# Linformer attention and a maxout feed-forward on one core: row maxima subtracted inside PSUM, and later keys transposed by TensorE

## The chip, the core and the metric

The kernel runs on one core of a Trainium2 chip. Times are microseconds (us) of device time for one execution. The kernel before takes 319.98 us (median of three runs, 319.91 to 320.13). TensorE appears in the profile as PE (matmuls) and PEld (weight loads), VectorE as DVE, ScalarE as ACT, GpSimd as POOL and SyncE as SP.

## The reference

```python
batch, n_heads, seq, head_dim = (8, 8, 1024, 64)      # k_proj = 64
def _attn_ref(q, k, v, E, F):
    k_proj = np.einsum('ks,bhsd->bhkd', E, k)
    v_proj = np.einsum('ks,bhsd->bhkd', F, v)
    scores = q @ k_proj.transpose(0, 1, 3, 2) / np.sqrt(q.shape[-1])
    scores = scores - np.max(scores, axis=-1, keepdims=True)
    attn = np.exp(scores)
    attn = attn / (np.sum(attn, axis=-1, keepdims=True) + 1e-09)
    return np.matmul(attn, v_proj)

# x: attention's output as 8192 tokens by 512
def _moe_ref(x, w1, w2, w_out):                       # 512x1024, 512x1024, 1024x512
    return np.maximum(x @ w1, x @ w2) @ w_out
```

The query of a token is compared with 64 projected keys, so a row of scores has 64 entries. The row's maximum cancels in the quotient; it only bounds the argument of the exponential.

## The kernel before

The kernel goes through the 8 batches. A batch's attention is cut into four *groups* `(g, j)`: four heads (`g`) by half the tokens (`j`), `W` = 256 columns each for even and odd tokens (`o`). The feed-forward works on *units* `(b, o)`, two per batch. Both matrix products of a unit use seven block products instead of eight (`p1` to `p7`, in `up_steps` for the first product and `down_steps` for the second). Most `up` products are copied to SBUF by ACT (`keep`, L676) or combined by DVE (`add`, L717), and the block sums that the next products need are formed by DVE (L662). `max(x@w1, x@w2) @ w_out` is computed with the difference of the two weights (`wd_sb`) and a relu, plus `x` times a product of weights (`m_sb`).

One group of attention is:

- `score` (L327): 16 small matmuls of 64 rows by 32 columns, `kpt` (keys, transposed) against `qt` (queries, transposed), 256 columns moving. The result has keys over partitions and tokens along the row, in two PSUM banks.
- an exponential on ACT out of PSUM (`scores`, L427; `step_sc`, L374 for the first groups). No maximum is subtracted.
- `sums_into` and `values_into` (both through `tiles_into`, L346): denominators (8 small matmuls with ones) and weighted values (16).
- logarithm and exponential of the negative on ACT (L448, L452), which gives the reciprocal of the denominators, and one multiply on DVE (L456) that writes the group's part of `xt`.

In the steady part `step_group` (L409) issues the scores of one group right beside denominators and values of the group before. `step_later` hands out the rest: logarithm, reciprocal, multiply.

Keys and values are projected in `step_kv` (batch 0, and batches 3 to 7 with `dma=True`) or `step_kv_sets` (batches 1 and 2). For batches 3 to 7 the projected keys are copied twice side by side and transposed by a DMA on SP's queue (`step_kpt_dma`, L291); batches 1 and 2 transpose on TensorE (`step_kpt_sets`, L254) and copy with one DVE instruction (L258). Queries are transposed by TensorE for batches 0 and 1 (`step_qt`, L305, copied by DVE at L310) and by DMA on SP's queue after that (`step_qt_dma`, L317). On POOL's queue a one-element copy from a transposed tile (`step_gate`, L297) holds back the loads of the next batch until the transposes by DMA are done.

PSUM has eight banks: four single ones named `mm0` to `mm3` (`mm_bank`) and two pairs with the tag `att` (`att_banks`).

The order of all work is written out by hand. The list `slots` holds the feed-forward's pieces in the order in which they are issued, each with a key: `("U", n, h, i)` is the `i`-th up product of half `h` (a half holds seven of them) while unit `n` does its down products, `("P", n, p, i)` a piece of down product `p`, `("G", n, h)` the start of a half, where `step_group` sits. `at_slot` hangs a step of attention behind such a key. A step that returns a function has it called after the next slot: that is how a copy out of PSUM is issued one slot behind its matmuls. Each engine takes its instructions in this order.

A batch covers two units, hence four halves, hence four groups. Units 3, 5, 7, 9 and 11 (`kv_units`) begin with the projection of keys and values of batches 3 to 7.

Of the kernel before, what the change touches and what calls it, by code (L numbers as in the profile page):

```python
# [16 lines left out]
def kernel(  # L17
# [33 lines left out]
    soft = ctx.enter_context(tc.tile_pool(name="soft", bufs=5))  # L51
    opool = ctx.enter_context(tc.tile_pool(name="opool", bufs=14))
    ppool = ctx.enter_context(tc.tile_pool(name="ppool", bufs=4))
# [52 lines left out]

    tiles = {b: {} for b in range(B)}
    for n in ("k", "q", "v"):
# [45 lines left out]


    eft = [const.tile([128, NC, KP], FP16, tag=f"eft{i}", name=f"eft{i}") for i in range(2)]

# [12 lines left out]
    def new_attn(t):  # L170
        t["kp"] = proj.tile([KP, H, 2, D], FP16, tag="kp", name="kp_sb")
        t["vp"] = proj.tile([128, H, 2, D // 2], FP16, tag="vp", name="vp_sb")
        t["kpt"] = proj.tile([128, H, KP], FP16, tag="kpt", name="kpt_sb")
        t["qt"] = qtp.tile([128, H, HALF], FP16, tag="qt", name="qt_sb")


    def step_kv(t, h0=0, h1=H, which="kv", att=False, dma=False, copy=nc.vector.tensor_copy, between=None):
        kv_ps = att_banks()[:, 0, :] if att else mm_bank(n=0 if dma else None)
        n = (h1 - h0) * D
        both = which == "v"  # L180
        nh = 2 if both else h1 - h0
        for h in range(0, h1 - h0, nh):
            if h and between is not None:
                between()
            for c in range(NC):
                for w in which:
                    i = "kv".index(w)
                    for r in range(2) if both else (i,):
                        nc.tensor.matmul(  # L189
                            out=kv_ps[r * KP : (r + 1) * KP, h * D : (h + nh) * D],  # L190
                            lhsT=eft[i][:, c, :],
                            rhs=t[w][:, h0 + h : h0 + h + nh, c, :],
                            start=(c == 0), stop=(c == NC - 1),
                        )
        zd = lambda ap: ap.rearrange("p (h d z) -> p h z d", d=D // 2, z=2)
        if "k" in which:
            eng = nc.vector.tensor_copy if which == "k" or dma else nc.scalar.copy
            kp = t["kp"][:, h0:h1]
            eng(out=kp[:, :, 0, :], in_=kv_ps[0:KP, 0:n].rearrange("p (h d) -> p h d", d=D))
        if both:  # L200
            copy(out=t["vp"][:, h0:h1], in_=zd(kv_ps[:, 0:n]))
        elif "v" in which:
            def finish_v():
                nc.vector.tensor_copy(out=t["vp"][KP:128, h0:h1], in_=zd(kv_ps[KP:128, 0:n]))
                if dma:
                    nc.vector.tensor_copy(out=kp[:, :, 1, :], in_=kp[:, :, 0, :])
                    step_kpt_dma(t)
                else:
                    step_vp(t, h0, h1)

            if att:
                return finish_v
            finish_v()


    def step_vp(t, h0=0, h1=H):
        fl = lambda ap: ap[:, h0:h1].rearrange("p h z d -> p (h z d)")
        nc.vector.tensor_copy(out=fl(t["vp"][0:KP]), in_=fl(t["vp"][KP:128]))


    ORDER = (0, 2, 1, 3)

    def step_kv_sets(t):
        bank = att_banks()[:, 0, :]
# [12 lines left out]
        k_ps = bank[:, 0:n].rearrange("p (h d) -> p h d", d=D)  # L237
        nc.scalar.copy(out=kp[:, 0 : H // 2, :], in_=k_ps)
        nc.scalar.copy(out=kp[:, H // 2, :], in_=k_ps[:, 0, :])
# [9 lines left out]
        return finish_v  # L249

    def step_kpt_sets(t):
        kpt_ps = att_banks(FP16)[:, 0, :]
        for i, a in enumerate(ORDER):
# [3 lines left out]
            )  # L257
        nc.vector.tensor_copy(  # L258
            out=t["kpt"].rearrange("q h k -> q (h k)"), in_=kpt_ps[:, 0 : H * KP]
        )  # L260

    def kpt_of(t, head, o):
        rows = t["kpt"][o * D : (o + 1) * D]
        if "sets" not in t:
            return rows[:, head]
        s, m = divmod(head, H // 2)
        return rows[:, 2 * ORDER.index((m - o) % (H // 2)) + s]

# [6 lines left out]
    def step_kpt(t, h0=0, h1=H, att=False):  # L275
        kpt_ps = att_banks(FP16)[:, 0, :] if att else mm_bank(FP16)
        for h in range(h0, h1):
            for r in range(2):
                nc.tensor.transpose(
                    out=kpt_ps[r * D : (r + 1) * D, (h - h0) * KP : (h - h0 + 1) * KP],  # L280
                    in_=t["kp"][:, h, 0, :],
                    identity=ident16[:KP, :KP],
                )
        nc.vector.tensor_copy(
            out=t["kpt"][:, h0:h1, :].rearrange("q h k -> q (h k)"),
            in_=kpt_ps[:, 0 : (h1 - h0) * KP],
        )


    def step_kpt_dma(t):  # L290
        nc.sync.dma_start_transpose(  # L291
            out=t["kpt"], in_=t["kp"].rearrange("p h r d -> p (h r d)")
        )

# [30 lines left out]
    Z = D // 2  # L325

    def score(t, g, j, banks):  # L327
        for h in range(2):
            for o in range(2):
                for e in range(2):  # L330
                    head = 4 * g + 2 * h + e
                    for s in range(2):
                        pos = D * (o ^ e) + s * Z
                        nc.tensor.matmul(  # L334
                            out=banks[e][pos : pos + Z, h * W : (h + 1) * W],
                            lhsT=kpt_of(t, head, o)[:, s * Z : (s + 1) * Z],
                            rhs=t["qt"][o * D : (o + 1) * D, head, j * W : (j + 1) * W],
                            start=True, stop=True,
                        )
        t["ex", g, j] = soft.tile([128, 2, HALF], FP16, tag="soft", name="ex_sb")  # L340
# [582 lines left out]
    step_qt(t, 0, 4, NI // 2, NI)  # L923
    warm(2)
    step_sc(t, 0, 0)
    step_sc(t, 0, 1)
    warm(2)
    step_kv(t, 4, 8, "k")
    step_dn(t, 0, 0)
    warm(2)  # L930
    step_kpt(t, 4, 8)
    step_dn(t, 0, 1)
    step_inv(t, 0, 0)
    step_inv(t, 0, 1)
    warm(2)
    step_qt(t, 4, 4, 0, NI // 2)
    step_qt(t, 4, 4, NI // 2, NI)
    warm(2)
    step_sc(t, 1, 0)
    step_kv(t, 0, 2, "v")  # L940
    step_kv(t, 2, 4, "v")
    step_dn(t, 1, 0)
    step_sc(t, 1, 1)
# [96 lines left out]
    for n, x in enumerate((  # L1040
        "", "", "", "", "", "kv", "", "kpt", "qt00 qt10", "", "sc00 sc10", "qt01",
        "qt11 dn00 in00 dn10 in10", "", "", "at00 AT10 sc01",
    )):
        key = ("P", n // 15, (n - 1) // 2 % 7, (n - 1) % 2) if n else (0, 22)
        for name in x.split():
# [6 lines left out]
            else:  # L1052
                g, j = int(name[2]), int(name[3])
                s_ = {"qt": step_qt, "sc": step_sc,
                      "dn": step_dn, "in": step_inv, "at": step_at, "AT": step_at}[name[:2]]
                args = (4 * g, 4, 2 * j, 2 * j + 2) if name[:2] == "qt" else (g, j)
# [13 lines left out]
    at_slot(("U", 1, 0, 1), step_kv_sets, t)  # L1070
    at_slot(("U", 1, 0, 4), step_kpt_sets, t)
    at_slot(("P", 0, 6, 0), step_qt_dma, t, H // 2, H)
# [3 lines left out]
    for b in range(3, B):  # L1076
# [5 lines left out]
        at_slot(key, step_qt_dma, t, H // 2, H)  # L1082
        at_slot(("G", n, 0), step_kv, t, 0, H, "kv", False, True)
        at_slot(("U", n, 0, 2), step_vp, t)
        at_slot(("U", n, 0, 6), step_gate, t, "qt", H - 1)
        at_slot(("U", n, 0, 6), step_gate, t, "kp", H - 1, 1)
        at_slot(("U", n, 0, 6), loads, b + 1, "k", "v", "q")
    for n, h in (3, 1), (4, 0), (4, 1), (5, 1), (6, 0), (6, 1), (7, 1), (8, 0):
        at_slot(("U", n, h, 3), lambda: held.pop(0)())
    groups = [(tiles[b], g, j) for b in range(1, B) for j in range(2) for g in range(2)][2:]  # L1090
    none = (None, None, None)
    for i, (new, old) in enumerate(zip([*groups[1:], none], groups)):
        n, h = divmod(i + 2, 2)
# [72 lines left out]
```

## Time and profile before

| | |
|---|---|
| median of three runs | 319.98 us (319.91 to 320.13) |
| the profiled execution | 319.73 us, its span 318.0 us |
| ACT COPY L676, 128x512 f32 out of PSUM | 592 ns, 179 times |
| DVE TENSOR_TENSOR L717, 128x512, one operand in PSUM | 688 ns, 56 times |
| DVE TENSOR_TENSOR L456, 128x1024, one operand in PSUM | 1219 ns, 26 times |
| DVE TENSOR_TENSOR L662, 128x1024 f16 / 128x512 f16 | 683 / 419 ns |
| key transposes by DMA (`kpt_sb<-kp_sb`) | 5, 2.9 us each to landing |
| query transposes by DMA (`qt_sb<-q_sb`) | 12, 5.1 us each to landing |
| stores of the output | 256 KB each, 2.7 us to landing |

The busy time of a matmul in the profile overlaps with that of its neighbours, because matmuls are pipelined: a 256-column matmul is listed with 273 ns, but in a row of them one starts every 0.109 us. Paces are therefore read from the start times. A few per cent of matmul records can be missing. On DVE, too, a queued instruction starts a little before the listed end of the one before it. In the timeline a line shows its start, its length, the engine, the line of the kernel, the operation and the tiles, and in brackets how long the engine was idle before and for whom.

### The profile page before, as it was taken

Reading aid. Unit: us, or ns where it says so; the run is one execution under the profiler, and the core shown is the slowest. Engines: PE = TensorE matmul, PEld = TensorE weight load, DVE = VectorE, ACT = ScalarE, POOL = GpSimd, SP = SyncE. Lnnn points to the kernel's source line nnn. Section 1 sums busy time; section 2 is a strip of 40 time slices with the busy share of each in tenths; the row PEclk is TensorE's granted clock in tenths of the full one; section 3 lists DMA queues with packets and bytes.
Section 4 is the critical chain, followed back from the end, with each engine's and each line's share of the span. In section 5 each row is a group of like instructions: output and inputs, shape, how many; then the busy total and the mean of one; then the engine's idle time right before and its main releaser. Section 6 shows DMA issues by size and latency. Waiting matters only on the chain.

```text
span 318.0 us, 9177 instructions
## 1 busy us (share of the span) xinstructions
PE 312.1 (98%) x3920; PEld 253.5 (80%) x3920; DVE 240.4 (76%) x437; ACT 206.1 (65%) x372; POOL 40.0 (13%) x63
## 2 busy tenths in 40 slices
PE   8989999999999999999999999999999999999996
PEld 3555588788887888788887888788887888888885
DVE  2366888877969696996969696996969696969683
ACT  2476843777776777477776778477776777765541
POOL 8269002003000300030000400040000000000000
DMA  7999999999969899899989999989969131303124
GB/s 184 203 200 197 204 206 203 207 180 157 205 119 197 152 217 245 212 182 172 237 196 213 165 200 244 221 154 179 235 142 207 45 102 35 101 33 102 35 99 132
DMA packets 76424, 53.41 MB, mean 168 GB/s; under 512 B 29536, under 2 KB 76000, under 8 KB 76384
## 3 DMA queue, kind: packets, MB, share of 16 engines
q0 software_dynamic: 30688, 28.05, 56.4%
q1 hardware_dynamic: 45408, 24.58, 32.2%
q8 instruction: 30, 0.49, 0.6%
q10 hardware_dynamic: 288, 0.20, 0.2%
q14 instruction: 10, 0.08, 0.1%
HBM read 57.15 MB, written 16.78 MB: 233 GB/s over the span
## 4 chain that ended last, share of the span: by engine, by line
PE 92%; DMA 4%; POOL 1%; ACT 1%; DVE 0%; issue 0%; POOLq 0%; DVEq 0%
PE mm_ps L794 47%; PE mm_ps L702 27%; PE mm_ps L481 4%; DMA v_sb<-in_v_dram 4%; PE att_ps L346 3%; PE mm_ps L189 3%; PE mm_ps L334 2%; PE mm_ps L590 2%; PE att_ps L231 1%; PE mm_ps L305 1%; POOL k_sb L102 0%; POOL q_sb L102 0%; ACT ld_sb L382 0%; ACT ex_sb L374 0%; DVE o_sb L892 0%; PE att_ps L513 0%
## 5 line engine op out<-in xcount | busy, mean ns | idle before, releaser
L676 ACT COPY p_sb<-mm_ps 128x512 f32<-128x512 f32 x179 | 101.8, 592 | 49.4 <-PE mm_ps L702 27.6
L794 PEld LDWEIGHTS <-big 128*128 128x128 f16 x768 | 73.6, 98 | 11.8 <-issue 3.6
L794 PE MATMUL mm_ps<-T_sb,big 128*128 128x256 f16 x576 | 76.9, 273 | 0.0
L717 DVE TENSOR_TENSOR gt_sb<-mm_ps,p_sb 128x512 f16<-128x512 f32 x56 | 38.5, 688 | 43.9 <-PE mm_ps L702 43.6
L702 PE MATMUL mm_ps<-big,big 128*128 128x256 f16 x336 | 50.4, 273 | 0.0
L702 PEld LDWEIGHTS <-big 128*128 128x128 f16 x448 | 43.8, 98 | 5.1
L794 PE MATMUL mm_ps<-wo_sb,gt_sb 128*128 128x256 f16 x256 | 42.6, 273 | 0.0
L794 PEld LDWEIGHTS <-gt_sb 128*128 128x128 f16 x376 | 35.7, 98 | 6.7 <-issue 2.7
L427 ACT ACTIVATE ex_sb<-mm_ps 128x512 f16<-128x512 f32 x50 | 27.2, 596 | 18.0 <-PE mm_ps L334 12.3
L702 PEld LDWEIGHTS <-wd_sb 128*128 128x128 f16 x336 | 32.9, 98 | 3.8
L702 PE MATMUL mm_ps<-xt_sb,wd_sb 128*128 128x256 f16 x224 | 32.8, 273 | 0.0
L456 DVE TENSOR_TENSOR xt_sb<-att_ps,ld_sb 128x1024 f16<-128x1024 f32 x26 | 31.7, 1219 | 0.2
L794 PE MATMUL mm_ps<-m_sb,xt_sb 128*128 128x256 f16 x128 | 24.4, 273 | 0.0
L824 DVE TENSOR_TENSOR o_sb<-mm_ps,p_sb 128x512 f32<-128x512 f32 x32 | 21.9, 683 | 2.8 <-ACT p_sb L853 2.0
L297 POOL COPY junk<-qt_sb 1x1 f16<-1x1 f16 x6 | 1.5, 246 | 175.1 <-DMA qt_sb<-q_sb 175.1
L720 DVE TENSOR_SCALAR gt_sb<-gt_sb 128x512 f16<-128x512 f16 (+1 forms) x60 | 21.5, 359 | 2.1
L662 DVE TENSOR_TENSOR big<-gt_sb 128x1024 f16<-128x1024 f16 x32 | 21.9, 683 | 0.0
L794 PE MATMUL mm_ps<-wo_sb,big 128*128 128x256 f16 x128 | 21.5, 273 | 0.0
L763 ACT ACTIVATE gt_sb<-mm_ps 128x512 f16<-128x512 f32 x28 | 16.8, 601 | 5.7 <-PE mm_ps L702 5.7
L794 PE MATMUL mm_ps<-T_sb,gt_sb 128*128 128x256 f16 x120 | 20.3, 273 | 0.0
L794 PEld LDWEIGHTS <-xt_sb 128*128 128x128 f16 x188 | 18.3, 98 | 2.3 <-issue 0.2
L717 DVE TENSOR_TENSOR gt_sb<-p_sb 128x512 f16<-128x512 f32 x28 | 19.1, 682 | 0.6 <-ACT p_sb L676 0.6
(113 smaller groups left out, 432.3 us busy)
## 6 DMA issues: line engine op xcount, KB each, us to landing
out_dram<-o_sb SPq DMA_DIRECT2D x62, 256.0 KB, 2.7
k_sb<-in_k_dram POOLq DMA_DIRECT2D x7, 1024.0 KB, 10.6
v_sb<-in_v_dram POOLq DMA_DIRECT2D x7, 1024.0 KB, 16.6
q_sb<-in_q_dram POOLq DMA_DIRECT2D x5, 1024.0 KB, 23.5
q_sb<-in_q_dram POOLq DMA_DIRECT2D x6, 512.0 KB, 16.2
big<-in_moe_w_dram POOLq DMA_DIRECT2D x12, 128.0 KB, 6.6
v_sb<-in_v_dram POOLq DMA_DIRECT2D x4, 256.0 KB, 13.5
wo_sb<-in_moe_w_out_dram POOLq DMA_DIRECT2D x1, 1024.0 KB, 10.8
```

What stands on the lines that cost most here:

```text
L189: nc.tensor.matmul(out=kv_ps[r * KP : (r + 1) * KP, h * D : (h + nh) * D], lhsT=eft[i][:, c, :], rhs=t[w][:, h0 + h : h0 + h + nh, c, :], ...
L427: nc.scalar.activation(out=t["ex", g, j][:, e, :], in_=banks[e], func=ACTF.Exp, scale=scale)
L456: nc.vector.tensor_tensor(out=x_out(t, g, j).rearrange("q z o n -> q o z n"), in0=at_ps.rearrange("q o (z n) -> q o z n", z=2), in1=ld[:, ...
L481: nc.tensor.matmul(out=h_ps, lhsT=wd_sb[:, r, fb * 128 : (fb + 1) * 128], rhs=t["xt"][:, r, :, j * W : (j + 1) * W], start=(r == 0), stop= ...
L662: nc.vector.tensor_tensor(out=S(i), in0=S(0) if x is None else x, in1=y(), op=op)
L676: copy(out=x, in_=bank)
L702: nc.tensor.matmul(out=bank[:, m * W : (m + 1) * W], lhsT=w_[:, n_, (2 * d + m) * 128 : (2 * d + m + 1) * 128], rhs=a[:, n_, :], start=(n ...
L717: nc.vector.tensor_tensor(out=c_blk(j, c), in0=two(x), in1=two(y), op=ALU.add)
L720: nc.vector.tensor_scalar_max(ap, ap, 0.0)
L763: nc.scalar.activation(out=out, in_=in_, func=ACTF.Relu)
L794: nc.tensor.matmul(out=bank[i][:, 0:CH] if two_banks else bank[:, i * CH : (i + 1) * CH], lhsT=a(c)[:, i * 128 : (i + 1) * 128], rhs=w_(c) ...
L824: nc.vector.tensor_tensor(out=o_sb, in0=two(x), in1=two(y), op=ALU.add)
```

## The change

For each group the row maxima are now computed and subtracted before the exponential.

`step_top` computes the group's scores a second time in another form: `qt` is the stationary operand (128 tokens) and `kpt` moves, so that tokens lie over partitions and the 64 keys of a head lie along the row. For this `kpt` becomes a fixed tile with zeros: even tokens have their keys in one half of the columns, odd tokens in the other, so that one matmul of 128 rows and 128 columns gives both without mixing them. Eight matmuls fill two banks; two DVE reduces (one per bank) take the maxima into `top`, 128 tokens by up to 128 columns, of which eight are used.

`step_topt` transposes `top` with two TensorE transposes, and ACT copies the result to `topt`. In `score` sixteen more small matmuls follow the sixteen of before: they multiply `topt` with `pick`, which holds -1 in the row of the head, and add into the same PSUM columns.

The keys of batches 3 to 7 go through `step_kv_sets` and `step_kpt_sets`, as batches 1 and 2 did, with copies by DVE; the key transposes by DMA and their gate on POOL are dropped. `step_kpt_sets` copies into the zeroed tile with four DVE instructions in place of one. Output buffers go from 14 to 12. In batch 0 the steps are reordered by hand and two calls of `warm(2)` are dropped.

```diff
-    opool = ctx.enter_context(tc.tile_pool(name="opool", bufs=14))
+    opool = ctx.enter_context(tc.tile_pool(name="opool", bufs=12))
...
+    kpt_of_b = [const.tile([128, H, 2, KP], FP16, tag=f"kpt{i}", name=f"kpt{i}") for i in range(2)]
+    top = [const.tile([128, 2, 128], FP16, tag=f"top{i}", name=f"top{i}") for i in range(2)]
+    for x in kpt_of_b + top:
+        nc.vector.memset(x, 0.0)
+    pick = const.tile([128, 4, 32], FP16)
+    nc.vector.tensor_tensor(
+        out=pick, in0=ident16[:, 0:4, None].broadcast_to([128, 4, 32]),
+        in1=ident16[:, D : D + 4, None].broadcast_to([128, 4, 32]), op=ALU.add,
+    )
+    nc.vector.tensor_scalar_mul(pick, pick, -1.0)
...
     def step_kpt_sets(t):
...
-        nc.vector.tensor_copy(
-            out=t["kpt"].rearrange("q h k -> q (h k)"), in_=kpt_ps[:, 0 : H * KP]
-        )
+        def finish():
+            src = kpt_ps[:, 0 : H * KP].rearrange("q (y x s k) -> q x y s k", y=2, x=2, s=2)
+            dst = t["kpt"].rearrange("q (s x y) r k -> q r x y s k", s=2, x=2)
+            lo, hi = slice(0, D), slice(D, 128)
+            nc.vector.tensor_copy(out=dst[lo, 0], in_=src[lo])
+            nc.vector.tensor_copy(out=dst[hi, 1, :, 1], in_=src[hi, :, 0])
+            for x in range(2):
+                nc.vector.tensor_copy(out=dst[hi, 1, 1 - x, 0], in_=src[hi, x, 1])
+
+        return finish
...
-    def step_kpt_dma(t):
-        nc.sync.dma_start_transpose(
-            out=t["kpt"], in_=t["kp"].rearrange("p h r d -> p (h r d)")
-        )
...
+    def step_top(t, g, j):
+        first = t is tiles[0]
+        pair = None if first else att_banks()
+        banks = [mm_bank() if first else pair[:, i, :] for i in range(2)]
...
+        for i in range(2):
+            for h in range(4):
+                nc.tensor.matmul(
+                    out=banks[i][:, h * 128 : (h + 1) * 128],
+                    lhsT=t["qt"][:, 4 * g + h, j * W + i * 128 : j * W + (i + 1) * 128],
+                    rhs=t["kpt"][:, 4 * g + h].rearrange("q r k -> q (r k)"),
+                    start=True, stop=True,
+                )
+
+        def finish():
+            for i in range(2):
+                nc.vector.tensor_reduce(
+                    out=top[k][:, i, :].rearrange("p (o h) -> p h o", o=2)[:, 0:4, :],
+                    in_=banks[i].rearrange("p (h o k) -> p h o k", h=4, o=2),
+                    axis=mybir.AxisListType.X, op=ALU.max,
+                )
+
+        return finish
+
+    def step_topt(t, g, j):
+        x = t.pop(("top", g, j))
+        ps_t = mm_bank(FP16) if t is tiles[0] else att_banks(FP16)[:, 0, :]
+        for i in range(2):
+            nc.tensor.transpose(
+                out=ps_t[:, i * 128 : (i + 1) * 128], in_=x[:, i, :], identity=ident16
+            )
+        t["topt", g, j] = y = proj.tile([128, W], FP16, tag="topt", bufs=2, name="topt_sb")
+
+        def finish():
+            nc.scalar.copy(out=y, in_=ps_t[:, 0:W])
+
+        return finish
...
     def score(t, g, j, banks):
...
+        less = t.pop(("topt", g, j))
+        for shift in range(2):
+            for h in range(2):
+                for o in range(2):
+                    rows = slice(o * D, (o + 1) * D)
+                    for e in range(2):
+                        head = 4 * g + 2 * h + e
+                        for s in range(2):
+                            pos = D * (o ^ e) + s * Z
+                            nc.tensor.matmul(
+                                out=banks[e][pos : pos + Z, h * W : (h + 1) * W],
+                                lhsT=pick[rows, 2 * h + e, :] if shift
+                                else kpt_of(t, head, o)[:, s * Z : (s + 1) * Z],
+                                rhs=less[rows, :] if shift
+                                else t["qt"][rows, head, j * W : (j + 1) * W],
+                                start=(h == 0 and not shift), stop=bool(shift),
+                                skip_group_check=True,
+                            )
...
-        "", "", "", "", "", "kv", "", "kpt", "qt00 qt10", "", "sc00 sc10", "qt01",
-        "qt11 dn00 in00 dn10 in10", "", "", "at00 AT10 sc01",
+        "", "", "", "", "", "kv", "", "kpt", "qt00 qt10", "", "tp00 tp10", "tt00 tt10 qt01 qt11",
+        "sc00 sc10", "dn00 in00 dn10 in10", "tp01", "", "at00 AT10 tt01", "sc01",
...
-    at_slot(("U", 1, 0, 4), step_kpt_sets, t)
+    at_slot(("U", 1, 0, 3), step_kpt_sets, t)
...
-        at_slot(("G", n, 0), step_kv, t, 0, H, "kv", False, True)
-        at_slot(("U", n, 0, 2), step_vp, t)
+        at_slot(("G", n, 0), lambda t=t: step_kv_sets(t, mm_bank(n=0), nc.vector.tensor_copy))
+        at_slot(("U", n, 0, 1), step_kpt_sets, t)
         at_slot(("U", n, 0, 6), step_gate, t, "qt", H - 1)
-        at_slot(("U", n, 0, 6), step_gate, t, "kp", H - 1, 1)
...
+    at_slot(("P", 1, 0, 2), step_top, tiles[1], 1, 1)
+    at_slot(("P", 1, 1, 1), step_topt, tiles[1], 1, 1)
+    for i, (t, g, j) in enumerate(groups[1:]):
+        n, h = divmod(i + 1, 2)
+        first = (g, j) == (0, 0)
+        if n == 0:
+            continue
+        at_slot(("U", n, h, 4 + (n == 1) if first else 2), step_top, t, g, j)
+        at_slot(("U", n, h, 6 if first else 4), step_topt, t, g, j)
```

Counted over the kernel, each of the 32 groups gains 8 matmuls of 128x128 by 128, 2 transposes, 16 small matmuls, 2 DVE reduces and one ACT copy.

More of the change, by code (lines that the diff above doesn't have):

```diff
@@ L105, in load @@
         )
-    tiles = {b: {} for b in range(B)}
+    tiles = {b: {"b": b} for b in range(B)}
     for n in ("k", "q", "v"):
@@ L170, in new_attn, with step_kv @@
     def new_attn(t):
-        t["kp"] = proj.tile([KP, H, 2, D], FP16, tag="kp", name="kp_sb")
+        t["kp"] = proj.tile([KP, H, D], FP16, tag="kp", name="kp_sb")
         t["vp"] = proj.tile([128, H, 2, D // 2], FP16, tag="vp", name="vp_sb")
-        t["kpt"] = proj.tile([128, H, KP], FP16, tag="kpt", name="kpt_sb")
+        t["kpt"] = kpt_of_b[t["b"] % 2]
         t["qt"] = qtp.tile([128, H, HALF], FP16, tag="qt", name="qt_sb")
-    def step_kv(t, h0=0, h1=H, which="kv", att=False, dma=False, copy=nc.vector.tensor_copy, between=None):
-        kv_ps = att_banks()[:, 0, :] if att else mm_bank(n=0 if dma else None)
+    def step_kv(t, h0, h1, which, att=False, copy=nc.vector.tensor_copy, between=None):
+        kv_ps = att_banks()[:, 0, :] if att else mm_bank()
         n = (h1 - h0) * D
         both = which == "v"
+        i = "kv".index(which)
         nh = 2 if both else h1 - h0
@@ L185, in step_kv @@
             for c in range(NC):
[L186 to L193, printed above, removed]
-                        )
@@ L195, in step_kv @@
[L195 to L199, printed above, removed]
-        if both:
[L201 to L213, printed above, removed]
@@ L216, in step_vp @@
-    def step_vp(t, h0=0, h1=H):
-        fl = lambda ap: ap[:, h0:h1].rearrange("p h z d -> p (h z d)")
-        nc.vector.tensor_copy(out=fl(t["vp"][0:KP]), in_=fl(t["vp"][KP:128]))
+                for r in range(2) if both else (0,):
+                    nc.tensor.matmul(
+                        out=kv_ps[r * KP : (r + 1) * KP, h * D : (h + nh) * D],
+                        lhsT=eft[i][:, c, :],
+                        rhs=t[which][:, h0 + h : h0 + h + nh, c, :],
+                        start=(c == 0), stop=(c == NC - 1),
+                    )
@@ L221, with step_kv_sets @@
+        if both:
+            copy(
+                out=t["vp"][:, h0:h1],
+                in_=kv_ps[:, 0:n].rearrange("p (h d z) -> p h z d", d=D // 2, z=2),
+            )
+        else:
+            nc.vector.tensor_copy(
+                out=t["kp"][:, h0:h1, :], in_=kv_ps[0:KP, 0:n].rearrange("p (h d) -> p h d", d=D)
+            )
     ORDER = (0, 2, 1, 3)
-    def step_kv_sets(t):
-        bank = att_banks()[:, 0, :]
+    def step_kv_sets(t, bank=None, copy=nc.scalar.copy):
+        late = bank is None
+        if late:
+            bank = att_banks()[:, 0, :]
@@ L237, in step_kv_sets @@
         k_ps = bank[:, 0:n].rearrange("p (h d) -> p h d", d=D)
-        nc.scalar.copy(out=kp[:, 0 : H // 2, :], in_=k_ps)
-        nc.scalar.copy(out=kp[:, H // 2, :], in_=k_ps[:, 0, :])
+        copy(out=kp[:, 0 : H // 2, :], in_=k_ps)
+        copy(out=kp[:, H // 2, :], in_=k_ps[:, 0, :])
         def finish_v():
@@ L247, in finish_v @@
                 nc.vector.tensor_copy(out=vp[a : a + KP, m:H], in_=vp[b : b + KP, 0:m])
-        return finish_v
+        if late:
+            return finish_v
+        finish_v()
     def step_kpt_sets(t):
@@ L257, in step_kpt_sets @@
             )
-        nc.vector.tensor_copy(
-            out=t["kpt"].rearrange("q h k -> q (h k)"), in_=kpt_ps[:, 0 : H * KP]
-        )
-    def kpt_of(t, head, o):
[L263 to L267, printed above, removed]
+        def finish():
[7 more added lines that the diff above has]
+        return finish
+    def kpt_of(t, head, o):
+        return t["kpt"][o * D : (o + 1) * D, head, o, :]
     def vp_of(t, head, rows, z):
@@ L280, in step_kpt @@
                     out=kpt_ps[r * D : (r + 1) * D, (h - h0) * KP : (h - h0 + 1) * KP],
-                    in_=t["kp"][:, h, 0, :],
+                    in_=t["kp"][:, h, :],
                     identity=ident16[:KP, :KP],
                 )
[L284 to L287, printed above, removed]
-    def step_kpt_dma(t):
-        nc.sync.dma_start_transpose(
-            out=t["kpt"], in_=t["kp"].rearrange("p h r d -> p (h r d)")
-        )
+        for r in range(2):
+            rows = slice(r * D, (r + 1) * D)
+            nc.vector.tensor_copy(
+                out=t["kpt"][rows, h0:h1, r, :],
+                in_=kpt_ps[rows, 0 : (h1 - h0) * KP].rearrange("q (h k) -> q h k", k=KP),
+            )
     def step_gate(t, n, *at):
@@ L325 @@
     Z = D // 2
-    def score(t, g, j, banks):
[L328 to L339, printed above, removed]
+    top_turn = [0, 1]
@@ new lines, in step_top @@
+    def step_top(t, g, j):
+        first = t is tiles[0]
+        pair = None if first else att_banks()
+        banks = [mm_bank() if first else pair[:, i, :] for i in range(2)]
+        k = top_turn.pop(0)
+        top_turn.append(k)
+        t["top", g, j] = top[k]
+        for i in range(2):
[5 more added lines that the diff above has]
+                    start=True, stop=True,
+                )
+        def finish():
[4 more added lines that the diff above has]
+                    axis=mybir.AxisListType.X, op=ALU.max,
+                )
+        return finish
@@ new lines, in step_topt @@
+    def step_topt(t, g, j):
[4 more added lines that the diff above has]
+                out=ps_t[:, i * 128 : (i + 1) * 128], in_=x[:, i, :], identity=ident16
+            )
+        t["topt", g, j] = y = proj.tile([128, W], FP16, tag="topt", bufs=2, name="topt_sb")
+        def finish():
+            nc.scalar.copy(out=y, in_=ps_t[:, 0:W])
+        return finish
+    def score(t, g, j, banks):
+        less = t.pop(("topt", g, j))
[7 more added lines that the diff above has]
+                            pos = D * (o ^ e) + s * Z
+                            nc.tensor.matmul(
+                                out=banks[e][pos : pos + Z, h * W : (h + 1) * W],
[5 more added lines that the diff above has]
+                                skip_group_check=True,
+                            )
@@ L924 @@
     warm(2)
+    step_top(t, 0, 0)()
+    step_top(t, 0, 1)()
+    step_kv(t, 4, 8, "k")
+    step_topt(t, 0, 0)()
     step_sc(t, 0, 0)
+    step_topt(t, 0, 1)()
     step_sc(t, 0, 1)
     warm(2)
-    step_kv(t, 4, 8, "k")
+    step_kpt(t, 4, 8)
     step_dn(t, 0, 0)
     warm(2)
-    step_kpt(t, 4, 8)
+    step_qt(t, 4, 4, 0, NI // 2)
+    step_qt(t, 4, 4, NI // 2, NI)
     step_dn(t, 0, 1)
@@ L934 @@
     step_inv(t, 0, 1)
[L935 to L939, printed above, removed]
+    step_top(t, 1, 0)()
+    step_top(t, 1, 1)()
     step_kv(t, 0, 2, "v")
     step_kv(t, 2, 4, "v")
+    step_topt(t, 1, 0)()
+    step_sc(t, 1, 0)
+    step_topt(t, 1, 1)()
     step_dn(t, 1, 0)
@@ L1054 @@
                 s_ = {"qt": step_qt, "sc": step_sc,
-                      "dn": step_dn, "in": step_inv, "at": step_at, "AT": step_at}[name[:2]]
+                      "tp": step_top, "tt": step_topt, "dn": step_dn, "in": step_inv, "at": step_at, "AT": step_at}[name[:2]]
                 args = (4 * g, 4, 2 * j, 2 * j + 2) if name[:2] == "qt" else (g, j)
```

## The prediction

> **What bounds the kernel now.** I read the page's busy times and its chain first, then the windows by stage, the list of waits, and the timeline of one batch.
>
> ```profile
> span 318.0 us, 9177 instructions
> PE 312.1 (98%) x3920; PEld 253.5 (80%) x3920; DVE 240.4 (76%) x437; ACT 206.1 (65%) x372; POOL 40.0 (13%) x63
> ...
> PE 92%; DMA 4%; POOL 1%; ACT 1%; DVE 0%; issue 0%; POOLq 0%; DVEq 0%
> ```
>
> ```profile
> 203.50:239.00 35.50, 35.50 (x459) 29.69 (x459) 28.59 (x51) 24.88 (x46) 3.30 (x5) 1.00 0.98 183
> ```
>
> The last line is one batch of the steady part (columns: stretch, length, then busy time of PE, its loads, DVE, ACT, POOL, and the granted clock, DMA share and GB/s). TensorE is busy all of it, at clock 1.00, so whatever TensorE must issue or wait for in addition is paid in full. DVE has 7 us of slack per batch, and the list of waits says where it lies:
>
> ```profile
> DVE gt_sb L717 <- PE mm_ps L702: 43.6, 23, 3.0
> ```
>
> DVE idles until the second up product (p2), then has a backlog. A group is a quarter batch (35.5/4 = 8.9 us). In the third one:
>
> ```profile
> 224.67 0.60 PE L702 MATMUL mm_ps<-xt_sb,wd_sb 128*128 128x256 f16 x4
> ...
> 225.38 0.69 DVE L717 TENSOR_TENSOR gt_sb<-mm_ps,p_sb 128x512 f16<-128x512 f32 x1 [0.53 <-PE mm_ps L702]
> ...
> 226.92 0.68 DVE L662 TENSOR_TENSOR big<-gt_sb 128x1024 f16<-128x1024 f16 x1
> ...
> 227.29 0.60 PE L702 MATMUL mm_ps<-big,big 128*128 128x256 f16 x4
> 227.52 1.22 DVE L456 TENSOR_TENSOR xt_sb<-att_ps,ld_sb 128x1024 f16<-128x1024 f32 x1
> ...
> 228.65 0.68 DVE L662 TENSOR_TENSOR big<-gt_sb,big 128x1024 f16<-128x1024 f16 x1
> ```
>
> p2 is issued at 224.67, p7 at 227.29. DVE takes the sum after the long normalizing multiply at 228.65, after TensorE has passed p7. TensorE doesn't mind now, because nothing it needs comes from there.
>
> **The change, part by part.** *Matmuls added.* Per group: eight 128x128 by 128 for the second scores, two transposes of the maxima, sixteen small 64x32 by 256 that subtract. Their pace is in the chain:
>
> ```profile
> 52.60 0.89 PE mm_ps L305 x16
> ...
> 54.81 0.56 PE att_ps L334 x32
> ```
>
> ```profile
> 107.12 0.45 PE att_ps L346 x24
> ```
>
> Sixteen 128-wide transposes take 0.89, 0.0556 each: eight are 0.445, two 0.11. 32 small ones take 0.56 and 24 take 0.45, so 8 more cost 0.11, and sixteen 0.22 (the rest, 0.12, is paid once per burst). Sum 0.77 a group, 24.8 for 32 groups. An unusual pair of 128 columns can't be below the transpose's 0.0556; from above I bound it by a 256-column matmul (four in 0.44, 0.109). I take 0.0556, the same shape.
>
> The Trainium skill, "TensorE: Matmul & The Clock Gate", section "Back-to-back issue gap", says that a stream of load and matmul pairs 128 wide sustains about 81 ns a pair, which speaks against the change. The transposes here are such pairs at 55.6 ns, so the trace differs; by the page, ten pairs a group would add 32 x 10 x 0.025 = 8 us more (an estimate).
>
> *Keys of batches 3 to 7.* Sixteen 512-column matmuls (1.85 in the chain) become 32 of 256 columns, which is what batches 1 and 2 have (L231 x32, 1.87): nothing. Four transposes a batch come in, 0.22. On DVE, copies of 0.68, 0.69, 0.29 and 0.29 (1.95) make way for nine smaller ones, 2.65 by the lengths of L243, L247 and L258 (0.42, 0.22, 0.42): 0.7 more, all in the batch's first group, after which DVE idles 2.6 before the next p2. Five key transposes by DMA leave SP's queue and five gates (0.25 each) leave POOL's; the next loads start that much earlier, and nothing waits for them.
>
> *A wait on ACT.* In the built order those four transposes stand right behind p2 and take the PSUM buffer that the denominators hold until their logarithm (L448). That is behind two exponentials and two copies on ACT:
>
> ```profile
> 206.53 1.04 PE L702 MATMUL mm_ps<-xt_sb,wd_sb 128*128 128x256 f16 x8
> ...
> 207.69 0.64 ACT L448 ACTIVATE ld_sb<-att_ps 128x512 f32<-128x512 f32 x1
> ```
>
> p1 and p2 are over for TensorE 8 x 0.109 after their first load at 206.42, at 207.29; the logarithm ends at 208.33. The subtraction delays both alike. TensorE waits 1.05 a batch, and all of it queues behind.
>
> *A wait on DVE, the dear one.* The maxima are transposed right behind p7, in three of four groups, and need two DVE reduces first, which stand in DVE's order just where the sum of 228.65 stands. A reduce of 512 f32 values from PSUM isn't in the trace. Nearest are L717 and L824, 0.68 long but 0.60 apart when queued (226.32 to 226.92). Bounds: 0.34 apart (f16 sums of 512, 0.42 long) and 0.70 (the slowest 512 or 1024 wide f16 scalar operation, 0.77 long). I take 0.60, as it reads the same source. Third group: reduces end at 228.65 + 0.60 + 0.68 = 229.93; TensorE is past p7 at 227.73, plus 0.445 for the second scores that stand before it: 228.17. Wait 1.75. In the second group DVE gets there at 220.45, TensorE passes p7 at 219.42: 221.73 less 219.87 is 1.86. In the fourth 237.28 and 236.37: 238.56 less 236.81, 1.75. I take 1.8. In the first group of a batch the transposes stand four up and down steps later and by the same walk are 0.2 late enough: nothing. If that cover goes, it is 0.6 a batch.
>
> Each wait is new every group, since DVE is again idle at the next p2 (0.5 to 3.0 us before L717); 3 x 6 groups of batches 2 to 7: 32.4.
>
> The skill (same page, "The HAM clock gate") has the clock halve after an idle window of about 3.4 us. These waits are shorter, and the window above has 1.00; no run here shows the other.
>
> *Batch 2's first group* has the wait otherwise: second scores behind four key copies and the multiply (0.55), then reduces behind two adds and a relu (1.85): 2.4.
>
> *Batch 1.* Two groups at once: TensorE waits for two reduce pairs and a copy between (0.35 + 1.1), for the second exponential (0.9), for a copy queued behind both inversions (1.1); with small ones 3.6, and 3.1 of matmuls: 6.7. Bounds 3.1 and 9.
>
> *Batch 0, the start.* Before, the last denominators (L346) run at 21.30. After: query copies end 12.47, four reduces 14.9, shift of the first scores 15.0, exponential to 16.4, the second group's maxima copied on ACT only behind it (16.75), exponential to 18.2; query transposes 18.5 to 19.4, their copies to 20.3, four reduces to 22.7; v products wait for the reduces' banks to 22.3; scores 23.25, exponential 24.4, copy 24.75, scores 25.2, exponential 26.4, denominators 26.5. That is 5.2 later, and 0.4 comes back where TensorE waited for L497 at 27.62: 4.8. Bounds 2.5 and 6. Two matmul pairs for warming less are inside it. The zero fills on DVE (some 2 us) lie in its 3.2 us wait before L167.
>
> *Two output buffers less*: at nothing. A store lands in 2.7 us, a buffer comes back after four tiles, 17 us; without that cover DVE would wait with a store.
>
> **Sum.** A steady batch: 4 x 0.77 + 0.22 + 1.05 + 3 x 1.8 = 9.75, five times 48.8. Batch 2: 3.1 + 2.4 + 5.4 = 10.9. Batch 1 6.7, start 4.8. Total 71.2. The profiled execution took 319.73 (span 318.0 and 1.7 around it), 0.25 below the median of 319.98: 319.73 + 71.2 = 391.
>
> **Rivals.** (1) *No waits, matmuls alone.* DVE reaches the reduces in time, because a reduce is cheap and ACT and DVE have slack on average (28.6 and 24.9 of 35.5). Then 319.73 + 24.8 + 1.1 + 1.7 of the start = 347. Against it: the order is fixed, and DVE is late by 1.8 where a free reduce saves 1.2 at most. (2) *Dearer instructions.* A 128-wide product paced like a 256 one adds 0.53 a group, of which 0.43 is given back in the eighteen waits (17 less 7.7), and reduces at 0.70 add 0.2 x 18: 391 + 9.3 + 3.6 = 404. Nothing speaks for it but that both are unseen. (3) *The other side: the transfers set the pace.* The DMA share is 0.98 in the window above. If TensorE's matmuls hid waits for loads, added ones would fill them, and five key transposes (2.9 each to landing) would come back: 319.7 - 14.5 = 305. It decides if TensorE's waits for DMA beyond the start were over 71 us. The chain has DMA at 4%, all before 18.8. That the change doesn't do what it says is out: all its instructions stand in the built order.
>
> **How the numbers follow.** Forecast 391, chance 0.75, by itself 379 (reduces at 0.34: eighteen times 0.52 less, and 2 in the start) to 398. Rival 1 0.12, rival 2 0.10, rival 3 0.03. The range runs from 374, some way to rival 1, to 405, past rival 2; 0.17 is left out. A measurement here tells 0.2% from no change. Faster 0.02, same 0.01 (both rival 3), slower 0.97.
>
> **What would show it.** Right: a steady batch of 45.3 instead of 35.5 with PE's clock at 1.00; PE waits of the maxima's transposes for the reduces, about 1.8 each, eighteen times, and of the key transposes for the logarithm, 1 us, five times; second scores at 0.45 per eight; reduces 0.60 apart; the last denominators of batch 0 at 26.5. Wrong: PE busy without such gaps (rival 1), eight second scores in 0.9 (rival 2), or a wait of TensorE on DMA in the steady part.

## The result, and the profile after

The kernel after takes 394.66 us (median of four runs, 392.8 to 395.63), the one before 320.06 beside it (319.91 to 322.69): 1.23 times as long, 95% interval 1.2221 to 1.2379. The profiled execution took 392.8 us, its span is 391.0, 73.0 more than before. Predicted were 391.

The page of the kernel after: its span, busy times, and the chain's shares by engine.

```profile
span 391.0 us, 11159 instructions
...
PE 347.3 (89%) x4848; PEld 282.6 (72%) x4848; DVE 284.5 (73%) x540; ACT 218.3 (56%) x404; POOL 38.4 (10%) x58
...
PE 64%; DVE 24%; ACT 5%; DMA 4%; issue 2%; DVEq 0%; POOLq 0%; ACTq 0%
```

TensorE was busy for 98% of the span, now for 89%, and DVE has gone from 0% to 24% of the chain, though its own busy share fell from 76% to 73%. That is a wait on an engine that is not full.

The windows of the kernel after, one steady batch (columns as before: stretch, length, busy time of PE, its loads, DVE, ACT and POOL, clock, DMA share, GB/s):

```profile
256.50:301.65 45.15, 40.07 (x582) 33.78 (x584) 33.71 (x64) 26.43 (x50) 2.81 (x4) 1.00 0.80 145
```

45.15 long with PE busy 40.07; before it was 35.50 with PE busy 35.50. The clock is 1.00 in both. The DMA share fell from 0.98 to 0.80, so the transfers don't set the pace.

The list of waits of the kernel after (engine, line and tile that waited, for whom: us in total, times, longest), and the costliest group of reduces:

```profile
DVE gt_sb L764 <- PE mm_ps L749: 62.8, 39, 4.0
PEld L358 <- DVE top L346: 37.8, 43, 1.7
PE att_ps L358 <- DVE top L346: 28.5, 40, 1.4
...
PEld L254 <- issue: 4.9, 5, 1.0
PE att_ps L254 <- ACT ld_sb L495: 4.0, 5, 0.8
```

```profile
L346 DVE TENSOR_REDUCE top<-att_ps 128x8 f16<-128x512 f32 x56 | 36.0, 691 | 1.4 <-PE att_ps L337 1.4
```

The maxima's transposes (L358) wait for the reduces (L346). A load of weights and its matmul wait in the same gap, so the two L358 lines are not added. The five waits of the key transposes (L254) for the logarithm (L495) are there too. The first line is the other face: DVE idles 62.8 us (43.6 before) until the second up product gives it its next sum.

One such wait in the chain of the kernel after (start, length, what):

```profile
227.21 0.70 DVE gt_sb L764
...
228.14 1.22 DVE xt_sb L503
229.36 1.20 DVE o_sb L871 x2
230.55 1.22 DVE top L346 x2
...
231.82 0.23 PE att_ps L358
```

and the same in the timeline, on DVE and on TensorE's weight loads (in brackets, how long it was idle):

```profile
230.47 1.29 DVE L346 TENSOR_REDUCE top<-att_ps 128x8 f16<-128x512 f32 x2
231.67 0.42 DVE L709 TENSOR_TENSOR big<-xt_sb 128x512 f16<-128x512 f16 x1
...
229.46 0.43 PEld L749 LDWEIGHTS <-big 128*128 128x128 f16 x4
231.21 0.10 PEld L358 LDWEIGHTS <-top 128*128 128x128 f16 x1 [1.33 <-DVE top L346]
231.81 0.10 PEld L358 LDWEIGHTS <-top 128*128 128x128 f16 x1 [0.50 <-DVE top L346]
```

From the sum after p2 to the second reduce DVE works without a pause; TensorE has nothing left in front of the transposes after 230.0. By their starts two reduces take 1.20 together (230.47 to the next instruction at 231.67), 0.60 each, though the group view lists 691 ns for one.

By stage, from the starts of the key and value projections in the two chains (before: 48.44, 65.47, 96.96, then every 35.52; after: 54.38, 78.56, 121.04, then every 45.15):

| stage | before | after | more | predicted |
|---|---|---|---|---|
| start, up to batch 1's projection | 48.44 | 54.38 | 5.9 | 4.8 |
| batch 1 | 17.03 | 24.18 | 7.2 | 6.7 |
| batch 2 | 31.49 | 42.48 | 11.0 | 10.9 |
| batches 3 to 6, each | 35.52 | 45.15 | 9.63 | 9.75 |
| batch 7 and the end | 78.96 | 89.37 | 10.4 | 9.75 |

### The profile page after: what moved, and what is told of

Its sections match the earlier page's. It is cut to its first block, busy times and chain, and to the rows that moved or that the text cites. A ratio compares the mean times of both kernels' runs of the same rounds, so it can differ in the third digit from the quotient of the medians.

```text
span 391.0 us, 11159 instructions
## 1 busy us (share of the span) xinstructions
PE 347.3 (89%) x4848; PEld 282.6 (72%) x4848; DVE 284.5 (73%) x540; ACT 218.3 (56%) x404; POOL 38.4 (10%) x58
## 4 chain that ended last, share of the span: by engine, by line
PE 64%; DVE 24%; ACT 5%; DMA 4%; issue 2%; DVEq 0%; POOLq 0%; ACTq 0%
PE mm_ps L841 29%; PE mm_ps L749 13%; DVE top L346 7%; DVE xt_sb L503 6%; DVE o_sb L871 5%; DVE gt_sb L764 4%; PE mm_ps L528 4%; PE mm_ps L378 3%; PE att_ps L393 2%; PE mm_ps L229 2%; DMA out_dram<-o_sb 2%; ACT p_sb L723 2%; DMA k_sb<-in_k_dram 2%; PE mm_ps L637 2%; PE att_ps L358 1%
## 5 line engine op out<-in xcount | busy, mean ns | idle before, releaser
L723 ACT COPY p_sb<-mm_ps 128x512 f32<-128x512 f32 x179 | 102.3, 592 | 76.7 <-PE mm_ps L749 41.4
L764 DVE TENSOR_TENSOR gt_sb<-mm_ps,p_sb 128x512 f16<-128x512 f32 x56 | 38.7, 690 | 69.7 <-PE mm_ps L749 62.8
L841 PEld LDWEIGHTS <-big 128*128 128x128 f16 x768 | 72.1, 98 | 10.8 <-issue 3.4
L749 PEld LDWEIGHTS <-big 128*128 128x128 f16 x448 | 43.8, 98 | 5.1
L358 PE MATMUL att_ps<-ident,top 128*128 128x128 f16 x56 | 11.4, 227 | 29.0 <-DVE top L346 28.5
L346 DVE TENSOR_REDUCE top<-att_ps 128x8 f16<-128x512 f32 x56 | 36.0, 691 | 1.4 <-PE att_ps L337 1.4
L358 PEld LDWEIGHTS <-top 128*128 128x128 f16 x64 | 5.6, 96 | 38.6 <-DVE top L346 37.8
L503 DVE TENSOR_TENSOR xt_sb<-att_ps,ld_sb 128x1024 f16<-128x1024 f32 x26 | 31.7, 1220 | 0.2
L364 ACT COPY topt_sb<-att_ps 128x256 f16<-128x256 f16 x28 | 10.5, 375 | 20.1 <-PE att_ps L358 20.1
```

Of the source, the lines that this page charges most:

```text
L346: nc.vector.tensor_reduce(out=top[k][:, i, :].rearrange("p (o h) -> p h o", o=2)[:, 0:4, :], in_=banks[i].rearrange("p (h o k) -> p h o k" ...
L358: nc.tensor.transpose(out=ps_t[:, i * 128 : (i + 1) * 128], in_=x[:, i, :], identity=ident16)
L503: nc.vector.tensor_tensor(out=x_out(t, g, j).rearrange("q z o n -> q o z n"), in0=at_ps.rearrange("q o (z n) -> q o z n", z=2), in1=ld[:, ...
L723: copy(out=x, in_=bank)
L749: nc.tensor.matmul(out=bank[:, m * W : (m + 1) * W], lhsT=w_[:, n_, (2 * d + m) * 128 : (2 * d + m + 1) * 128], rhs=a[:, n_, :], start=(n ...
L764: nc.vector.tensor_tensor(out=c_blk(j, c), in0=two(x), in1=two(y), op=ALU.add)
```

## The experiments

Twelve kernels, all edits of the kernel after. "Steady batch" is the distance between two such projections. Where the clock matters it is given.

**1. Transposes of the maxima later.**

```diff
-        at_slot(("U", n, h, 6 if first else 4), step_topt, t, g, j)
+        at_slot(("U", n, h, 6), step_topt, t, g, j)
```

> The maxima's transposes of the eighteen waiting groups stand behind the seventh up product instead of the fifth, four products of 0.44 later on TensorE. Theory (TensorE waits there only because the two reduces end 1.75 after it arrives): the wait is covered, 18 x 1.6 to 1.75 come back, 363 to 367, and the steady batch falls from 45.15 to about 40. Rival (DVE as a whole is too slow, the wait only moves to the shift, the exponential or the next sum): 385 to 395.

365.68 (364.88 to 368.88), ratio to before 1.1451 (1.1391 to 1.1512); steady batch 40.41. 29 us come back from the transposes of eighteen groups, moved by 1.75 each. The rival falls: DVE does the same work in the same order.

**2. No reduces in three groups of four.**

```diff
-            for i in range(2):
+            for i in range(0 if t["b"] > 1 and (g, j) != (0, 0) else 2):
                 nc.vector.tensor_reduce(
```

> The two reduces are left out in the second to fourth group of batches 2 to 7 (these groups then subtract old maxima); all matmuls, transposes and copies stay. Theory: the wait of 1.75 goes, the multiply that also frees the PSUM buffer ends just before TensorE arrives, 394.7 - 18 x 1.75 = 363. Rival (the transposes would wait for the multiply and the two adds anyway): at most 18 x 1.2 saved less, 380 or more. Rival (the added matmuls are the cost): 394 unchanged.

361.05 at clock 1.00; steady batch 39.83, 5.32 less, that is 1.77 for each of three groups. All added matmuls are still there, so they are not the price: what the transposes waited for is the reduces. The multiply and the adds ahead of these are still in DVE's queue, and TensorE doesn't wait for them; they only made the reduces late (2.4 in the chain above).

**3. Key transposes one product later.**

```diff
-        at_slot(("U", n, 0, 1), step_kpt_sets, t)
+        at_slot(("U", n, 0, 2), step_kpt_sets, t)
```

> The four key transposes of batches 3 to 7 stand behind the third up product instead of the second, 0.87 later on TensorE. Theory (they wait 1.0 for the logarithm that frees their buffer): 0.15 of wait is left, 5 x 0.9 = 4.4 come back, 390, unless the key copies, now behind the multiply on DVE, make the second scores wait: then 0.3 to 0.8 of each is lost again. Rival (ACT's chain is late for the next exponential anyhow): 394.5, no change.

396.5 (395.05 to 399.97), ratio 1.2403 (1.2339 to 1.2468); steady batch 45.40, 0.25 longer. The wait on the logarithm is gone, and another has its place. The chain of this kernel:

```profile
222.00 1.22 DVE xt_sb L503
223.22 0.60 DVE o_sb L871
223.81 0.32 DVE kpt L262
...
224.15 0.29 DVE kpt L263
224.44 0.29 DVE kpt L265 x2
...
224.78 0.61 PE att_ps L337 x8
```

The key copies (L262 to L265) now stand behind the long multiply on DVE, and the second scores (L337) wait for them. I had put that loss at 0.3 to 0.8 a batch; the list of waits has it at 5.8 in six waits, 1.0 on average (the kernel after has one such wait, of 0.5).

**4. Second scores twice.**

```diff
-        for i in range(2):
+        for i in (0, 1, 0, 1):
             for h in range(4):
```

> The eight matmuls of the second form of the scores are issued twice in every group. Theory (0.0556 a matmul; where the transposes wait for DVE, TensorE has 1.75 to spare and the second set is hidden): only the fourteen groups without that wait pay, 14 x 0.445 = 6.2, 401. Rival (TensorE is the bound throughout, no wait to hide it): 32 x 0.445 = 14.2, 409. Rival (a 128-wide product of this kind costs as much as a 256-wide one): 14 x 0.87 = 12, 407, and eight of them take 0.9 in the chain.

397.27 at clock 1.00; the span is 395.5, 4.5 more than that of after. A steady batch is 45.75, 0.60 longer, where four groups would be 1.78: the first group pays (its sixteen take 0.89 in the chain), in the other three the second set lies in the wait:

```profile
222.60 0.89 PE att_ps L337 x16
```

```profile
PE att_ps L358 <- DVE top L346: 20.3, 39, 1.0
```

The waits for the reduces shrink from 28.5 us to 20.3, by 8.2, where eighteen sets of 0.445 are 8.0: one for one, as they must if DVE sets their end. At the start the four groups cost 0.3 together where I had counted 1.8, but that is not clear of noise: the same start takes 54.15 to 55.32 us in the profiles of the kernel after and of 1, 2, 5, 6, 9 and 10.

**5. Later transposes, and the logarithm first.** On top of 1:

```diff
-        ln_later = (n, h) == (1, 1) or h == 0 and n in kv_units
+        ln_later = (n, h) == (1, 1)
```

> As the run with the later transposes, and in the first group of batches 3 to 7 the logarithm goes to ACT ahead of two copies of products instead of behind them. Theory (the key transposes wait 1.0 only because the logarithm stands behind the copies): it ends before TensorE is there, 5 x 1.0 come back from 365.7: 360.7, steady batch 39.4 against 40.4. Rival (ACT is the limit, the copies that are now 0.5 late make the second sum and a PSUM bank late): half is given back, 363; or, as with the later key transposes, all of it, 365.7.

368.15 (366.49 to 369.04); steady batch 40.84, 0.43 longer than in 1. The transposes of keys no longer wait; the chain of this kernel in the first group:

```profile
202.87 0.64 ACT p_sb L723
...
203.53 0.70 DVE gt_sb L764
...
208.25 1.22 DVE top L346 x2
...
209.52 0.23 PE att_ps L358
```

A copy of a product (L723) goes later on ACT, the sum (L764) that needs it goes later on DVE (it starts 5.06 after the batch's projection, in 1 it is 4.56), and further down the same queue so do the reduces (9.70 against 9.20). The rival "as with the later key transposes, all of it" was right, by another path: the transposes of the maxima in the first group, which were just covered while TensorE waited for the logarithm, now wait for the reduces.

**6. Reduces ahead of the multiply.** On top of 5:

```diff
-        at_slot(("U", n, h, 4 + (n == 1) if first else 2), step_top, t, g, j)
+        at_slot(("U", n, h, 4 + (n == 1) if first else 1), step_top, t, g, j)
```

> As the run before, and the second scores stand one product earlier, so that DVE takes the two reduces ahead of the long multiply. Theory (what is left in the third group is DVE's backlog after the second product, and it falls when reduces are done in DVE's idle time): the last wait of 0.6 a batch goes, 5 x 0.6 = 3 below the run before, about 357.7, steady batch 38.8 (35.52 + 4 x 0.77 + 0.22). Rival (DVE has as much to do as before, its order doesn't matter): no change against the run before. Rival (the multiply, now 1.2 later, frees its buffer too late for the next group): slower than it by 3 or more.

368.83 (366.71 to 369.12), steady batch 40.8: no change against 5. DVE idles until the sum after p2 in both; reduces ahead of the multiply or behind it, the same work follows that sum before the next sum frees a PSUM bank for the scores. In both chains 5.99 us lie between that sum and the next scores (214.78 to 220.77 in 5, 216.53 to 222.52 here). My theory missed.

**7. Keys alone.** With `shift` only 0 in `score`, as in 8, and

```diff
     def step_top(t, g, j):
+        return lambda: None
...
     def step_topt(t, g, j):
+        return lambda: None
```

> All of the maxima is left out (second scores, reduces, transposes, copies, subtraction); the keys of batches 3 to 7 stay with TensorE and the start keeps its new order. Theory: only four transposes and the wait on the logarithm are left, 5 x (0.22 + 1.05) = 6.4, and up to 1.5 at the start: 326 to 328, steady batch 36.8. Rival (the keys by TensorE or the nine DVE copies cost more than that): 335 or more. Rival (the transposes by DMA were what held the loads): 320 or less.

329.69; steady batch 36.73, 1.21 over before (predicted 1.27). The total is 1.7 over the forecast's upper end. Batch 1 takes 18.32, 1.3 more than before, where I had nothing; the start takes 50.77, 2.3 more, where I had up to 1.5. In this execution the clock fell to 0.50 for 3.4 us at the start; the same start takes 49.84 at clock 1.00 in 11, 0.9 less.

**8. No subtraction.**

```diff
-        for shift in range(2):
+        for shift in range(1):
...
-                                start=(h == 0 and not shift), stop=bool(shift),
+                                start=(h == 0 and not shift), stop=True,
```

> The sixteen subtracting matmuls of each group are left out, the maxima are still formed. Theory (0.22 a group, none of it beside a wait): 394.7 - 32 x 0.22 = 387.6. Rival (the sixteen are as dear as the first sixteen of scores with their 0.34 together): 394.7 - 10.9 = 383.8. Rival (the waits of the maxima hide them): 394, unchanged.

386.47 at clock 0.996; steady batch 44.27, 0.88 less: 4 x 0.22, as counted.

**9. Logarithm first, no reduces in batches 2 to 7.** As 5, with the transposes at their old place.

```diff
-            for i in range(2):
+            for i in range(0 if t["b"] > 1 else 2):
                 nc.vector.tensor_reduce(
```

> The reduces are left out in all groups of batches 2 to 7 (stale maxima are subtracted there), and the logarithm of the first group goes ahead of the two copies. Theory (the key transposes' wait on the logarithm is real, but behind it stands DVE's work of the first group, which ends with the reduces; without these nothing follows): steady batch 35.52 + 4 x 0.77 + 0.22 = 38.8 against 39.84 without reduces in three groups, total 361.05 - 5 x 1.05 = 355.8. Rival (ACT itself is late: what the logarithm gives the two copies lose): 39.8 and 361.

354.79. The windows of this kernel, one batch:

```profile
192.08:231.02 38.94, 38.94 (x583) 33.83 (x584) 29.01 (x56) 26.05 (x50) 2.80 (x4) 1.00 0.92 183
```

TensorE is busy again for all of it. 38.94 is 35.52 and 3.42 of added matmuls (counted: 3.30). Against 2, 0.89 of wait on the logarithm went. What 3 and 5 could not get back is there as soon as DVE's queue behind it is shorter. Batch 2 becomes 2.06 shorter than in 2 as well: its first group waited for reduces.

**10. First group's maxima still later.** On top of 5:

```diff
-        at_slot(("U", n, h, 6), step_topt, t, g, j)
+        key = ("U", n, h, 6)
+        if first and n in kv_units:
+            order = [x for x, _ in slots]
+            key = order[order.index(("G", n, 1)) - 2]
+        at_slot(key, step_topt, t, g, j)
```

> As the run with later transposes and the logarithm first, and in the first group of batches 3 to 7 the maxima's transposes stand two more down pieces later, 0.87 on TensorE. Theory (DVE's reduces of the first group end 1.9 after TensorE would be there; that wait took the place of the one on the logarithm): 5 x 0.87 = 4.3 come back, steady batch 40.84 to 39.95, 363.8, about 2 under the run with later transposes alone. Rival (the subtraction then waits for ACT's copy, or the down products for their banks): 366 to 368.

368.39 (367.12 to 371.74); steady batch 40.88, no gain. The chain of this kernel, and its timeline, show the rival, one step earlier than I had put it:

```profile
209.85 0.59 ACT p_sb L723
210.44 0.28 ACT topt_sb L364
...
210.76 0.41 PE att_ps L393 x16
```

```profile
210.76 0.41 PE L393 MATMUL att_ps<-ex_sb,vp_sb 64*32 64x256 f16 x16 [0.71 <-ACT topt_sb L364]
```

The copy of the maxima (L364) now queues behind a copy of a product, and TensorE waits 0.7 for it: not at the subtraction, but at the weighted values (L393) ahead of it. By the code they need the pair of PSUM banks that the transposed maxima hold until that copy.

**11. Batch 0 without maxima.** In `step_top` and in `step_topt`, with no second pass of `score` for that batch:

```diff
+        if t is tiles[0]:
+            return lambda: None
```

> The maxima are left out in batch 0 alone. Theory (the start is 5.9 longer, of which 2.3 is its new order and the keys' second copy, as the run without any maxima has it, and 3.6 the maxima with their waits): the first projection of batch 1 starts at 50.8 instead of 54.4, and the total falls by 3.6 to 391. Rival (the maxima are hidden at the start by transfers of the first keys, queries and weights): within 1 of 394.7.

387.91 at clock 1.00; batch 1's projection starts at 49.84 instead of 54.38. So 4.5 of the start's 5.9 are the maxima and 1.4 its new order and the second copy of the keys. (My 2.3 came from 7 and holds its fall of the clock.) These are single profiles, and the start varies by up to 1.2 us between profiles of the same code (see 4).

**12. Idle stretches filled.** On top of 1:

```diff
     step_topt(t, 1, 1)()
+    warm(3)
     step_dn(t, 1, 0)
...
+        if (n, h) == (1, 0):
+            at_slot(("U", n, h, 6), warm, 6, True)
         at_slot(("U", n, h, 6), step_topt, t, g, j)
```

> As the run with later transposes, with matmuls of ones that nothing reads put into two stretches in which TensorE is mostly idle: three (0.27 each) behind the last maxima's transposes of batch 0, six ahead of the first maxima's transposes of batch 2, both in front of waits that cover them. Theory (in these stretches the granted clock sometimes falls to 0.50 for some 4 to 7 us, as at 87 to 91 in that run and at 27 to 33 in the run with later keys, because TensorE has been idle half of the time): the clock stays at 1.00 in nearly all executions, median 364.5 to 365 with a spread under 1, against 365.7 with 364.9 to 368.9. Rival (the clock's falls have nothing to do with the gaps): the same spread of 364.9 to 369, clocks from 0.986 up. Rival (the added matmuls are not covered): 367 or more at clock 1.00.

365.06 (364.19 to 365.22, five runs at clock 0.999 or 1.000), ratio 1.1397 (1.1379 to 1.1415). The spread went from 4.0 to 1.0 us. It was not run beside 1, so chance is not wholly out; kernels 5, 6 and 10, on the same chip, had a clock of 0.995 or less in seven runs of twelve. By its median this is the fastest form with maxima that was run (1, at clock 1.000, took 364.88); the kernel before, without them, stays far ahead.

## Why the prediction was right

- *The wait on DVE* (1.8 in eighteen groups, 32.4): shown. Runs 1 and 2 price it at 29 and at 31.7 (spans 391.0 and 359.3), 1.77 a group. A reduce, unseen before, takes 0.60 by the starts, which is what I had taken from instructions that read the same kind of source.
- *Added matmuls* (0.77 a group): shown. 9 leaves matmuls alone at 3.42 a batch with the key transposes, against 3.30; 8 prices the subtraction at 0.22 a group.
- *The wait on ACT* (1.05 a batch): 0.89 between 2 and 9. But it can't be had alone: in 3 and 5 a wait on DVE of the same size took its place. I had called the first group's transposes of maxima 0.2 late enough; that cover existed only because TensorE waited for the logarithm first.
- *Keys by TensorE* (0.22, nothing on DVE that shows): 7 has 1.21 a batch with the wait, as counted.
- *Batch 2* (2.4 in its first group): 2.06 by the reduces (2 to 9).
- *Batch 1* (6.7): 7.2. 7 without any maxima has 18.32 there, so 1.3 of it is the new order, where I had 0.9 for the late second exponential. The split of the rest was not tested.
- *The start* (4.8): 5.9, mis-sized (5.7 to 6.9 over the seven profiles named in 4). The walk holds to a few tenths until the scores of the fourth group (predicted 25.2, measured 24.99); the step that failed is "denominators 26.5". The exponential ends at 26.57, but they run at 27.39: TensorE first waits 0.76 ahead of weighted values and projects half of the v's in front of them.
- *Two output buffers less*, at nothing: no wait on a store appears among the long waits. Fourteen were not tried.
- *The rivals*: matmuls alone would be 347; without the waits of batches 2 to 7, 9 still takes 354.79, because the start and batch 1 keep theirs (6.6 and 7.2 over before, where their matmuls are 3.1 each). Dearer instructions are out by 4 and 8. Transfers as the pace are out by the DMA share of 0.80.

The sum of 71.2 stands against 73.0 measured at clock 1.00. The median lies 1.9 above the profiled execution; the other three runs had clocks of 0.991 to 0.996. That the clock would not fall is what the prediction got wrong in kind; the last section has it.

## What to carry to other kernels

Where engines run in a hand-written order, cost a new dependency by walking both queues to the point where they meet; average slack says nothing (DVE has 11 us of it in a batch of 45). Moving the consumer behind what the producer still has to do can be worth more than a cheaper instruction: here one edited line gave 29 us, where reduces that cost DVE nothing would have given at most 18 x 1.2 = 21.6 (an estimate). And a wait removed in front of another that it was hiding gives nothing: look for what was covered by it before you take it away.

## What the runs showed that I had not expected

The clock does fall in these kernels, in some executions, and in the profiles that show it always right after a stretch in which TensorE is partly idle: the first group of batch 2 (runs 1, 3, 6 and 8), the end of batch 0 (3 and 7), and once a wait for reduces near the end (3, at 350). Windows of run 1, then of run 12:

```profile
83.90:87.60 3.70, 1.52 (x17) 0.95 (x15) 3.46 (x8) 0.96 (x2) 0.00 (x0) 0.95 1.23 204
...
87.60:91.00 3.40, 3.40 (x67) 2.15 (x67) 0.00 (x0) 0.83 (x2) 0.00 (x0) 0.55 1.24 207
```

```profile
84.00:92.00 8.00, 7.12 (x109) 5.05 (x107) 4.23 (x10) 3.94 (x8) 0.00 (x0) 1.00 1.24 207
```

TensorE is busy 1.52 of 3.70 us, in pieces, with no gap over 1.4; then the granted clock falls to 0.50 for about 3.4 us. In run 3 it does so at the end of batch 0 for twice as long:

```profile
27.00:33.00 6.00, 5.54 (x75) 2.73 (x70) 4.52 (x10) 1.50 (x3) 5.15 (x6) 0.50 1.33 201
```

The profiled execution of the kernel after has the same stretch (1.52 busy of 3.70, from 84.20) at clock 1.00. So chance has a part in it, and part of that chance is where the stretch lies in time. In the traces of 1, 3, 6, 7 and 8 every fall named above begins a whole number of 3.413 us after the clock first rose to 1.00 (in run 1 it rose at 5.30 and fell at 87.22, 24 of them later). In the 3.41 us that end at these falls PE is busy 1.28 to 1.69 us. On the grid of the kernel after, the same stretch is cut elsewhere, into a span with 1.88 and the next; run 1 first, then the kernel after:

```profile
83.81:87.22 3.41, 1.49 (x16) 0.88 (x13) 3.33 (x9) 1.05 (x2) 0.00 (x0) 1.00 1.22 202
```

```profile
83.42:86.84 3.42, 1.88 (x20) 1.32 (x18) 3.34 (x9) 1.67 (x3) 0.00 (x0) 1.00 1.24 203
```

Busy time alone doesn't settle it: in run 10 the span from 84.04 to 87.45 has 1.65, and the clock stays at 1.00. With the first two stretches filled, in 12, the clock did not fall there. The price of a fall is not well known: 1.7 us for 3.4 at half clock if TensorE has work throughout (an estimate); in 1 the executions at 0.995 took 0.6 and 1.0 us more than the one at 1.000, in 6 those at 0.995 took 1.9 and 2.4 more. The kernel before has such executions too: 322.93 us at clock 0.995 and 324.22 at 0.989, of the seven beside 9, 10 and 11.

The Trainium skill ("TensorE: Matmul & The Clock Gate", "The HAM clock gate") has a free-running window of about 3.4 us, and halves the clock of an array that was idle for one. The length and the grid agree; that a window with PE up to half busy (1.69 of 3.41) can count as idle is what these runs add. The prediction had dismissed the gate because each wait was shorter than the window: several short ones close together are enough.
